# A fused attention, DFT and MLP kernel: front-end steps, weight sums and the start of TensorE's fixed order moved by a few matmul groups

## The chip, the cores and the metric

One core of one Trainium2 chip. The core's engines run side by side, each through its own queue in order: TensorE (PE) for matrix products, VectorE (DVE), ScalarE (ACT) and GpSimd (POOL) for elementwise work, SyncE (SP), which issues nearly all the DMAs here. The metric is the device time of one execution in microseconds; lower is better.

## What is computed

Pooled attention over 8 batches and 8 heads, then per batch a two-dimensional Fourier transform of which only the real part is kept, a layer norm, and an MLP of 512, 2048 and 512 channels.

```python
# q, k, v: (8, 8, 576, 64); pool = 8; w_ch1: (512, 2048); w_ch2: (2048, 512)
k_p = k.reshape(B, H, Sp, pool, D).mean(axis=3)
v_p = v.reshape(B, H, Sp, pool, D).mean(axis=3)
scores = scale * np.matmul(q, k_p.transpose(0, 1, 3, 2))
scores = scores - np.max(scores, axis=-1, keepdims=True)
attn = np.exp(scores)
attn = attn / (np.sum(attn, axis=-1, keepdims=True) + 1e-09)
attn_out = np.matmul(attn, v_p)            # -> x: (8, 576, 512)
...
X = np.fft.fft(np.fft.fft(x, axis=1), axis=2)
u = x + np.real(X).astype(np.float32)
mu = np.mean(u, axis=-1, keepdims=True)
var = np.mean((u - mu) ** 2, axis=-1, keepdims=True)
un = (u - mu) / np.sqrt(var + 1e-06)
return u + np.maximum(un @ w_ch1, 0.0) @ w_ch2
```

## The kernel before

**Two streams of work.** The MLP runs over nine blocks of 512 tokens, 4608 tokens in all; since a batch has 576 tokens, each block takes its tokens from two neighbouring batches, the last of one and the first of the next. The generator `fast()` yields the MLP's matmuls in 920 groups, mostly four to six matmuls each; a group's number is called its position here. Blocks 0 and 1 (`plain`, from positions 0 and 93) multiply the normalised tokens with the first weight in split precision: twelve matmuls into one PSUM tile g (L889), on the high part un0h, the low part un0l and un0h again; relu on ACT gives hh, DVE gives the low part hl (L895), and the second product collects in acc0 to acc3 (L853). From block 2 on (position 189, 104 positions to a block) the first product is made by a scheme with seven half-size products in place of eight (x, L957), which DVE adds up (sx, L918); ACT makes relu and hh (L926, L927), POOL hl (L928).

**The front end.** `fe(b)` is a generator too: all that batch b needs before its tokens can enter the MLP. In its order: pooling of k and v as trees of adds on POOL (L360); scores psS on TensorE (L432), their maxima mx on DVE (L434), the exps on ACT (L439); transposes psT, psV, psR; attention times values, psX (L516), which ACT copies into the batch's tile U (L518, L519) and DVE adds up in pairs (L526, L527); even and odd parts tmpE (L610) and tmpO (L623), split into high and low parts f (L600, L602); the transform's products psA (L644), psB (L661), psQ and psP; the mean psM (L755 to L760), the variance psVar (L806 to L825), the inverse root and the multiplication X (L833); and last the MLP's operands, un0l and un1l, on DVE and POOL (L725, L736, L739).

**What joins them.** The front end is cut into some 48 steps by its `yield`s. A table (AT for batches 4 to 7, AT3, AT2 and AT1) gives for each step the position behind which it is emitted, counted from the start of a block (`start`, `places`, `advance`). A step that is emitted sooner stands sooner on every engine on which its instructions run. MANUAL is the position from which TensorE executes exactly in the order in which the program is written; before it, and on the other engines all along, a scheduler sets the order.

**Weight sums.** The scheme of blocks 2 to 8 needs sums and differences of weight blocks. `combine(j)`, j from 0 to 7, makes them in one tile sx: four adds on DVE over the pair loaded from DRAM (L230 to L233), a high part on ACT (L236) and a low part on POOL (L237) for each of two halves, four stores to w1s (L239), and behind them the load of the next pair (L224) into the tile that the stores have just read. PAIRS gives their positions.

**Buffers.** PSUM has eight banks. Four are acc0 to acc3. Until block 0 is written, the others are two for g and two for the front end; then the program closes that pool and opens one ring of four that g, x and the front end share in turn. A tile takes the next bank of the ring, and waits until what was in it has been read. Weight tiles of the stream go round in a ring of twelve, loaded up to nine ahead by SP. Three tiles U hold batches in turn, `Us[b % 3]`; `evict` adds acc into U and sends it out (L874 to L879).

Of the kernel before, what the change touches and what calls it, by code (L numbers as in the profile page):

```python
# [52 lines left out]

RES = [0, 3, 6, 9, 11, 14]

UNITS0, UNITS, MANUAL, TAIL = 90, 104, 92, (2, 8, 14, 20, 26)
PAIRS = [97 + 11 * n for n in range(8)]
AT = [-64, -58, -56, -52, -50, -38, -36, -33, -31, -28, -26, -8, -6, 13, 14, 15, 16, 17, 18, 21, 22, 25, 26, 27, 28, 28,
      40, 41, 44, 46, 48, 49, 52, 52, 53, 55, 57, 59, 65, 66, 66, 79, 80, 80, 81, 82, 82, 104]
AT3 = [-46, -40, -38, -34, -32, -20, -18, -15, -14, -11, -9, -6, -4, 13, 14, 15, 16, 17, 18, 21, 22, 25, 26, 27, 28, 28,  # L60
      40, 41, 44, 46, 48, 49, 52, 52, 53, 55, 57, 59, 65, 66, 66, 79, 80, 80, 81, 82, 82, 104]
AT2 = [-6, 2, 4, 6, 8, 17, 18, 21, 22, 23, 24, 26, 27, 28, 29, 30, 31, 33, 34, 37, 38, 41, 42, 43, 44, 44,
       53, 54, 56, 57, 59, 60, 61, 61, 62, 64, 65, 66, 69, 70, 70, 79, 80, 80, 80, 81, 81, 100]
AT1 = [-1] * 7 + [2 + 3.5 * n for n in range(17)] + [93, 101, 113, 116, 117, 117, 117]
E0, O0, E1, O1 = 0, 1, 2, 3

HB = BLK // 2
# [17 lines left out]
def tile_kernel(ctx: ExitStack, tc: tile.TileContext, qt, kt, vm, vr, w1, w2, cad, cbd, mkd, out):  # L85
# [180 lines left out]
    def feed(look):  # L266

        while flow[1] < min(len(items), flow[0] + look):
            x = items[flow[1]]
            t = fresh("w1op" if x[0] in "ap" else "w2high" if x[0] == "h" else "w2low")  # L270
            if x[0] == "p":
                nc.sync.dma_start(raw(t), w1p[:, x[1], x[2]])
            elif x[0] != "a":
                nc.sync.dma_start(raw(t), (w2d if x[0] == "h" else w2l)[:, x[2]])
            else:
                src = w1s[:, x[2], x[3] - 3] if x[3] > 2 else w1p[:, 2 * x[2] + x[3] // 2, :, (x[3] > 0) * HB:(x[3] > 0) * HB + HB]
                nc.sync.dma_start(raw(t).rearrange("p (a n) -> p a n", a=2), src)
            tiles[x] = t
            flow[1] += 1
# [720 lines left out]
    def prep_next():  # L1000
        prep_w(done[0])
        done[0] += 1
# [4 lines left out]
        return UNITS0 + 96 * (k - 1) + (UNITS - 96) * max(0, k - 2) if k else 0  # L1007

    def places(c):
        return {1: AT1, 2: AT2, 3: AT3}.get(c, AT)  # L1010

    def advance(pos):
        for c in sorted(run):
            r = run[c]
            at = places(c)
            while r[1] < len(at) and pos >= at[r[1]] + start(c - 1):
                r[1] = len(at) - 1 if next(r[0], None) == "ln" else r[1] + 1
        c = max(run) + 1
        if c < B and pos + 1 >= places(c)[0] + start(c - 1):
            run[c] = [fe(c), 0]  # L1020
# [4 lines left out]
    for pos, _ in enumerate(fast()):  # L1025
        if pos % 3 == 2 and done[0] < min(len(pieces), AHEAD + pos // 3):
            prep_next()
        if pos in PAIRS:
            combine(PAIRS.index(pos))
        if pos in TAIL:  # L1030
            next(fe0, None)
        advance(pos)
        if done[0] == len(pieces):
            held = len(lows) + sum(i == 1 and f not in RES for i, f in highs)
            feed(LOOK if not held else min(LOOK, WBUFS - 3 - held))
        if pos + 1 == MANUAL:
            ctx.enter_context(tc.manual_schedule(engines={mybir.EngineType.PE}))
# [109 lines left out]
```

## Time and profile before

| | us |
|---|---|
| median of 3 runs | 1065.73 |
| lowest, highest run | 1061.01, 1066.77 |
| span of the profiled execution | 1062.5 |
| TensorE busy in it | 1004.7 (95%) |
| VectorE, ScalarE, GpSimd busy | 700.9 (66%), 567.1 (53%), 445.2 (42%) |

The profile was taken in one execution, of which the span is the time from its first to its last instruction; its whole time is not recorded apart, so the span is set beside the three timed runs. Busy times are read per engine: an engine that is busy for 95% of the span is short of work for 5% of it, and the views below say where. A row of the waits reads "line of the waiting instruction, from whose result it was released, total, times, longest". In a timeline a bracket at a row's end gives the idle time of the engine just before it and what ended that. The granted clock of TensorE is 1.00 at 2.4 GHz and 0.50 at 1.2 GHz.

### The profile page before, as it was taken

How to read it: one execution, taken by the hardware profiler on the slowest of the kernel's cores; microseconds unless marked ns; L12 is line 12 of the kernel's file. 1: busy time of each engine (PE TensorE's matmuls, PEld its weight loads, DVE VectorE, ACT ScalarE, POOL GpSimd, SP SyncE). 2: the span in 40 equal slices, each digit the busy share in tenths (PEclk: the TensorE clock that was granted, in tenths of full speed). 3: DMA queues.
4: the chain of work that ended last, by engine and by line, in shares of the span. 5: the costliest groups of instructions: out<-in, count | busy, mean ns of one | idle time of the engine just before them, and what ended most of it. 6: DMA issues, size and time to landing. Idle time of an engine off the chain costs nothing.

```text
span 1062.5 us, 18758 instructions
## 1 busy us (share of the span) xinstructions
PE 1004.7 (95%) x5982; PEld 868.1 (82%) x5982; DVE 700.9 (66%) x1387; ACT 567.1 (53%) x1687; POOL 445.2 (42%) x461
## 2 busy tenths in 40 slices
PE   6879999898898899999999999999999999999998
PEld 4656778677777789888998889889989998999997
DVE  6898686766579657866786667866785677223222
ACT  5768673565445655565557556566655344222221
POOL 5614433245533564357534753454352234222221
PEclk8989999899899999999999999999999999999999
DMA  8479997687755776777677767786777588988883
GB/s 274 176 236 393 357 326 245 200 258 242 244 158 151 248 253 197 244 248 260 206 236 256 246 194 232 236 268 202 219 224 242 168 247 258 298 256 261 290 257 136
DMA packets 161458, 256.11 MB, mean 241 GB/s; under 512 B 15952, under 2 KB 73296, under 8 KB 161104
## 3 DMA queue, kind: packets, MB, share of 16 engines
q1 hardware_dynamic: 161072, 252.24, 73.8%
q0 software_dynamic: 288, 2.66, 0.7%
q8 instruction: 49, 0.80, 0.3%
q14 instruction: 49, 0.40, 0.1%
HBM read 217.63 MB, written 37.22 MB: 240 GB/s over the span
## 4 chain that ended last, share of the span: by engine, by line
PE 66%; DVE 10%; DMA 9%; POOL 6%; ACT 5%; issue 3%; SPq 0%; POOLq 0%; DVEq 0%; ACTq 0%
PE acc L853 28%; PE x L957 21%; PE g L889 4%; PE psX L516 3%; DMA v<-in_vm 2%; DMA k<-in_kt 2%; ACT t L439 2%; PE psS L432 2%; PE psP L678 2%; DMA sx<-w1d 1%; PE psT L468 1%; PE psB L661 1%; DMA w1s<-sx 1%; PE psA L644 1%; POOL v L360 1%
## 5 line engine op out<-in xcount | busy, mean ns | idle before, releaser
L918 DVE TENSOR_TENSOR sx<-x,sx 128x256 f32<-128x256 f32 x336 | 154.5, 464 | 144.4 <-PE x L957 139.5
L928 POOL TENSOR_TENSOR hl<-sx,hh 128x512 fp32r<-128x512 f32 x112 | 153.9, 1374 | 222.3 <-ACT hh L927 196.5
L957 PE MATMUL x<-un0h,w1op 128*128 128x256 f32 x896 | 174.4, 282 | 0.2 <-ACT t L439 0.2
L853 PE MATMUL acc<-hh,w2low 128*128 128x512 f32 x576 | 165.1, 400 | 0.0
L926 ACT ACTIVATE sx<-sx 128x512 f32<-128x512 f32 x112 | 71.0, 634 | 156.9 <-DVE sx L918 154.8
L957 PEld LDWEIGHTS x<-un0h,w1op 128*128 128x128 f32 x896 | 143.4, 189 | 11.6 <-ACT t L439 0.4
L957 PE MATMUL x<-un1h,w1op 128*128 128x256 f32 x672 | 134.2, 281 | 2.7 <-DVE A L629 1.6
L957 PEld LDWEIGHTS x<-un1h,w1op 128*128 128x128 f32 x672 | 111.5, 188 | 17.0 <-DVE sx L918 3.0
L853 PEld LDWEIGHTS acc<-hh,w2low 128*128 128x128 f32 x576 | 101.2, 189 | 15.9 <-issue 0.4
L853 PE MATMUL acc<-hh,w2high 128*128 128x512 f32 x360 | 106.7, 405 | 0.0
L853 PE MATMUL acc<-hl,w2high 128*128 128x512 f32 x360 | 104.3, 399 | 2.3 <-POOL hl L928 2.3
L957 PE MATMUL x<-un0l,w1op 128*128 128x256 f32 x448 | 88.9, 280 | 3.3 <-DVE un0l L736 3.3
L439 ACT ACTIVATE t<-psS,mx 128x72 f32<-128x72 f32 x240 | 73.9, 333 | 17.9 <-DVE mx L434 17.5
L853 PEld LDWEIGHTS acc<-hl,w2high 128*128 128x128 f32 x360 | 63.2, 189 | 13.8 <-POOL hl L928 4.1
L853 PEld LDWEIGHTS acc<-hh,w2high 128*128 128x128 f32 x360 | 64.4, 192 | 9.4
L927 ACT CAST hh<-sx 128x512 fp32r<-128x512 f32 x112 | 69.8, 624 | 3.0
L957 PEld LDWEIGHTS x<-un0l,w1op 128*128 128x128 f32 x448 | 68.2, 188 | 3.8 <-DVE un0l L736 3.7
L360 POOL TENSOR_TENSOR v<-v 128x256 f32<-128x256 f32 (+1 forms) x56 | 53.7, 959 | 37.6 <-DMA v<-in_vm 36.7
L957 PE MATMUL x<-un1l,w1op 128*128 128x256 f32 x336 | 66.4, 279 | 1.1 <-POOL un1l L736 1.1
L853 PE MATMUL acc<-hl,w2h 128*128 128x512 f32 x216 | 61.3, 403 | 2.0 <-DVE hl L895 1.4
L448 POOL TENSOR_TENSOR t<-t,sm 128x720 f32<-128x720 f32 x30 | 45.3, 1512 | 42.7 <-DVE sm L447 21.4
L853 PE MATMUL acc<-hh,w2h 128*128 128x512 f32 x216 | 60.4, 399 | 1.8 <-ACT hh L927 1.2
(267 smaller groups left out, 2096.1 us busy)
## 6 DMA issues: line engine op xcount, KB each, us to landing
w1op<-w1s SPq DMA_DIRECT2D x224, 256.0 KB, 3.4
w1op<-w1p SPq DMA_DIRECT2D x200, 256.0 KB, 3.7
w2low<-w2l SPq DMA_DIRECT2D x128, 256.0 KB, 3.7
w2high<-w2d SPq DMA_DIRECT2D x80, 256.0 KB, 3.7
U<-in_w SPq DMA_DIRECT2D x16, 512.0 KB, 6.0
sx<-in_w SPq DMA_DIRECT2D x16, 512.0 KB, 5.9
w1s<-sx SPq DMA_DIRECT2D x32, 256.0 KB, 3.8
k<-in_kt SPq DMA_DIRECT2D x28, 288.0 KB, 3.3
```

The lines of the kernel that those rows point to most:

```text
L360: nc.gpsimd.tensor_tensor(out=out if n == 1 else src[:, :, 0:n], in0=src[:, :, 0] if n == 1 else src[:, :, 0:n], in1=src[:, :, 1] if n == ...
L432: nc.tensor.matmul(ps[:, c * W2J:(c + 1) * W2J], lhsT=q[:, r0:r0 + P], rhs=kpb[g % 2], start=True, stop=True)
L439: behind["S", b, gi, i] = nc.scalar.activation(t[:, c0 + c, h], pv[:, c, h], AF.Exp, bias=mx[x], accum_out=sm[x])
L448: ins = nc.gpsimd.tensor_tensor(out=t, in0=t, in1=sm.unsqueeze(3).broadcast_to([P, 5, 2, J]), op=ALU.mult)
L516: behind["X", b] = nc.tensor.matmul(ps, lhsT=w, rhs=a, start=(i == 0), stop=(i == len(mm) - 1))
L853: nc.tensor.matmul(acc[e], lhsT=a[:, e], rhs=h, start=(f == 0 and x == 0), stop=(f == NFC - 1 and x == 2))
L889: nc.tensor.matmul(ps, lhsT=w[:, c], rhs=x[:, ti], start=(n == 0), stop=(n == 11))
L918: nc.vector.tensor_tensor(out=o, in0=x, in1=y, op=ALU.add)
L926: nc.scalar.activation(c, c, AF.Relu)
L927: nc.scalar.copy(out=h, in_=c)
L928: nc.gpsimd.tensor_tensor(out=l, in0=c, in1=raw(h), op=ALU.subtract)
L957: nc.tensor.matmul(ps, lhsT=w[:, q, i], rhs=y[:, c + i], start=(n == 0), stop=(n == 5))
```

## The change

It moves the emission of steps; no instruction's work changes. MANUAL goes from 92 to 86. PAIRS, eight positions 11 apart, become a list in which sums 3 and 4 share position 136. AT1, AT2 and AT3 are rewritten, and AT is replaced by one table for each of the batches 4 to 7. Line numbers of the changed kernel are 8 higher than before.

```diff
-UNITS0, UNITS, MANUAL, TAIL = 90, 104, 92, (2, 8, 14, 20, 26)
-PAIRS = [97 + 11 * n for n in range(8)]
-AT = [-64, -58, -56, -52, -50, -38, -36, -33, -31, -28, -26, -8, -6, 13, 14, 15, 16, 17, 18, 21, 22, 25, 26, 27, 28, 28,
...
+UNITS0, UNITS, TAIL = 90, 104, (2, 8, 14, 20, 26)
+MANUAL = 86
+PAIRS = [95, 110, 119, 136, 136, 145, 158, 174]
+AT4 = [-64, -58, -56, -46, -46, -38, -36, -33, -31, -28, -27, -9, -7, 13, 15, 15, 16, 17, 18, 21, 22, 25, 26, 27,
...
     def places(c):
-        return {1: AT1, 2: AT2, 3: AT3}.get(c, AT)
+        return (None, AT1, AT2, AT3, AT4, AT5, AT6, AT7)[c]
...
-        if pos in PAIRS:
-            combine(PAIRS.index(pos))
+        for j, p in enumerate(PAIRS):
+            if p == pos:
+                combine(j)
```

In positions: batch 2's four score tiles of its first group of heads go from 92, 94, 96 and 98 to 96, 98, 98 and 98; its psA steps (s26 to s28) from 143, 144 and 146 to 142 for all; the steps with psM to the end by one up or down. Batch 3's score steps s9 to s12 go from 175, 177, 180 and 182 to 179 for all, its psX steps s13 to s16 from 199 to 202 to 199 for all, s21 to s25 from 211 to 214 to 207 for all; s28 stands at 221 (before 230) and s29 at 227 (before 232). In batches 4 to 7 the second pair of score steps stands 6 and 4 positions later, the middle of the transform one later, and the last six steps, at 79 to 82 of their block before, all at 76 now.

TensorE, where block 1 begins: psS_3 and psS_2 are score tiles of batch 2, g_1_0 the first tile of block 1. Before:

```order
L853 MATMUL acc_3_887<-hl,w2h 128x512
L432 MATMUL psS_3_0_1865<-kpb_79,q_3_1793 128x144 x3
L889 MATMUL g_1_0_1881<-un0h_870,w1op 128x512 x4
L889 MATMUL g_1_0_1881<-un0l_871,w1op 128x512 x4
L432 MATMUL psS_3_3_1901<-kpb_79,q_3_1793 128x144 x2
L889 MATMUL g_1_0_1881<-un0h_870,w1op 128x512 x4
L853 MATMUL acc_0_884<-hh,w2high 128x512
L853 MATMUL acc_0_884<-hh,w2low 128x512
L853 MATMUL acc_0_884<-hl,w2high 128x512
L853 MATMUL acc_1_885<-hh,w2high 128x512
L432 MATMUL psS_2_0_1954<-kpb_78,q_2_1807 128x144 x3
```

The first three score products stand ahead of g_1_0, two more inside it.

TensorE at the same place in the changed kernel:

```order
L861 MATMUL acc_3_887<-hl,w2h 128x512
L897 MATMUL g_1_0_1876<-un0h_850,w1op 128x512 x4
L897 MATMUL g_1_0_1876<-un0l_851,w1op 128x512 x4
L897 MATMUL g_1_0_1876<-un0h_850,w1op 128x512 x4
L861 MATMUL acc_0_884<-hh,w2high 128x512
L861 MATMUL acc_0_884<-hh,w2low 128x512
L861 MATMUL acc_0_884<-hl,w2high 128x512
L861 MATMUL acc_1_885<-hh,w2high 128x512
L440 MATMUL psS_3_0_1915<-kpb_79,q_3_1793 128x144 x3
```

After eight further products into acc, TensorE's order in the changed kernel goes on with the rest of the scores, the first tile of block 1's second piece of the hidden layer (g_1_1) and psVar of batch 1:

```order
L440 MATMUL psS_3_3_1938<-kpb_79,q_3_1793 128x144 x2
L440 MATMUL psS_2_0_1979<-kpb_78,q_2_1807 128x144 x3
L440 MATMUL psS_2_3_1990<-kpb_78,q_2_1807 128x144 x2
L897 MATMUL g_1_1_2059<-un0h_850,w1op 128x512 x4
L897 MATMUL g_1_1_2059<-un0l_851,w1op 128x512 x4
L814 MATMUL psVar_2072<-avg,lf 128x1 x5
```

The scores have gone from in front of and between the parts of g_1_0 to behind it, four tiles close together ahead of g_1_1, and psVar of batch 1 stands one third of g_1_1 sooner.

DVE, around weight sum 5 (the rows on sx are its four adds) and the psX adds of batch 2. Before:

```order
L526 TENSOR_TENSOR U_86<-psX_0_2540,U_86 128x288
L895 SCALAR_TENSOR_TENSOR hl<-g_1_6_2506,hh 128x512
L527 TENSOR_TENSOR U_86<-psX_0_2540,U_86 128x288
L526 TENSOR_TENSOR U_86<-psX_0_2551,U_86 128x288
L527 TENSOR_TENSOR U_86<-psX_0_2551,U_86 128x288
L610 TENSOR_TENSOR tmpE<-U_86 128x287
L410 SCALAR_TENSOR_TENSOR rw_80<-vt,mk,rw_80 32x63
L410 SCALAR_TENSOR_TENSOR rw_80<-vt,mk,rw_80 32x1
L616 TENSOR_TENSOR xt<-U_86 1x287
L623 TENSOR_TENSOR tmpO<-U_86 128x288
L526 TENSOR_TENSOR U_86<-psX_1_2566,U_86 128x288
L230 TENSOR_TENSOR sx<-sx 128x256
```

The sum's first add is the last of these rows.

DVE at that place in the changed kernel:

```order
L508 TENSOR_TENSOR R<-psR_1_2500,R 32x512
L903 SCALAR_TENSOR_TENSOR hl<-g_1_6_2495,hh 128x512
L534 TENSOR_TENSOR U_86<-psX_0_2531,U_86 128x288
L535 TENSOR_TENSOR U_86<-psX_0_2531,U_86 128x288
L238 TENSOR_TENSOR sx<-sx 128x256
L534 TENSOR_TENSOR U_86<-psX_0_2546,U_86 128x288
L239 TENSOR_TENSOR sx<-sx 128x256
L534 TENSOR_TENSOR U_86<-psX_1_2553,U_86 128x288
L535 TENSOR_TENSOR U_86<-psX_0_2546,U_86 128x288
L618 TENSOR_TENSOR tmpE<-U_86 128x287
```

The sum's first add has gone from behind both psX_0 adds, tmpE, xt, tmpO and the first psX_1 add to a place between the two pairs of psX_0 adds.

DVE, where the operands of block 2 are made (un0l_2295 before, un0l_2276 now; un0l_3420 belongs to block 3). Before:

```order
L434 TENSOR_REDUCE mx<-psS_1_0_3331 128x6
L447 RECIPROCAL sm<-sm 128x10
L736 TENSOR_TENSOR un0l_2295<-X,un0h_2294 128x4x192
L434 TENSOR_REDUCE mx<-psS_1_3_3354 128x4
L739 TENSOR_TENSOR X<-X 128x2x192 x4
L446 TENSOR_SCALAR sm<-sm 128x10
L447 RECIPROCAL sm<-sm 128x10
L895 SCALAR_TENSOR_TENSOR hl<-g_1_15_3366,hh 128x512
L736 TENSOR_TENSOR un0l_3420<-X,un0h_3419 128x4x96
L736 TENSOR_TENSOR un0l_2295<-X,un0h_2294 128x4x192
```

The second un0l_2295, the last row, stands behind hl and un0l_3420.

DVE there in the changed kernel:

```order
L903 SCALAR_TENSOR_TENSOR hl<-g_1_14_3276,hh 128x512
L442 TENSOR_REDUCE mx<-psS_0_0_3300 128x6
L442 TENSOR_REDUCE mx<-psS_0_3_3311 128x4
L744 TENSOR_TENSOR un0l_2276<-X,un0h_2275 128x4x192
L442 TENSOR_REDUCE mx<-psS_1_0_3327 128x6
L442 TENSOR_REDUCE mx<-psS_1_3_3338 128x4
L747 TENSOR_TENSOR X<-X 128x2x192 x3
L454 TENSOR_SCALAR sm<-sm 128x10
L747 TENSOR_TENSOR X<-X 128x2x192
L455 RECIPROCAL sm<-sm 128x10
L744 TENSOR_TENSOR un0l_2276<-X,un0h_2275 128x4x192
```

The block's second un0l has lost the other block's un0l and an hl in front of it, and two maxima of score tiles stand further forward.

## Rows read from the trace of the kernel before

**Rows 1.** The page's first line: the span of the profiled execution.

```profile
span 1062.5 us, 18758 instructions
```

**Rows 2.** Stretches: window, length, busy us by engine, TensorE's clock, DMA share, GB/s.

```profile
186.00:235.00 49.00, 41.91 (x203) 33.65 (x202) 35.00 (x77) 28.63 (x122) 16.80 (x15) 0.93 0.71 230
235.00:335.00 100.00, 90.09 (x452) 74.52 (x451) 66.93 (x130) 56.26 (x202) 45.14 (x53) 0.95 0.67 211
335.00:400.00 65.00, 57.53 (x373) 50.98 (x372) 41.37 (x91) 34.73 (x115) 36.30 (x45) 0.97 0.71 225
400.00:880.00 480.00, 471.62 (x3101) 424.29 (x3100) 348.80 (x688) 275.31 (x863) 220.48 (x215) 1.00 0.73 229
192.80:199.60 6.80, 4.01 (x10) 3.27 (x11) 4.04 (x10) 4.16 (x17) 4.01 (x4) 0.50 0.34 115
264.50:271.30 6.80, 3.33 (x11) 2.86 (x12) 4.91 (x7) 1.88 (x5) 4.87 (x7) 0.50 0.49 135
281.50:284.90 3.40, 3.40 (x13) 2.91 (x12) 2.25 (x5) 2.87 (x12) 3.24 (x5) 0.50 0.52 124
339.50:343.00 3.50, 3.50 (x11) 2.72 (x10) 2.55 (x10) 1.02 (x2) 1.31 (x1) 0.51 0.26 77
```

**Rows 3.** TensorE's waits, 180 to 1050 us: line, released by, total us, times, longest.

```profile
PE psA L644 <- DVE f L602: 4.7, 1, 4.7
PE g L889 <- ACT t L439: 4.5, 1, 4.5
PE x L957 <- DVE un0l L736: 3.3, 2, 3.0
PE acc L853 <- POOL hl L928: 2.9, 4, 1.0
PE psS L432 <- ACT t L439: 2.4, 1, 2.4
PE x L957 <- DVE A L629: 1.6, 1, 1.6
PE psX L516 <- ACT U L519: 1.6, 1, 1.6
PE psB L661 <- ACT f L600: 1.4, 1, 1.4
```

**Rows 4.** TensorE's timeline, 187 to 214 us: start, duration, instruction, idle before it and releaser.

```profile
195.59 2.08 PE L889 MATMUL g<-un0h,w1op 128*128 128x512 f32 x4 [4.51 <-ACT t L439]
197.46 1.91 PE L889 MATMUL g<-un0l,w1op 128*128 128x512 f32 x4
```

**Rows 5.** DVE's timeline, 186 to 197 us, the last un0l of block 1.

```profile
194.97 0.31 DVE L725 TENSOR_TENSOR un0l<-X,un0h 128x160 fp32r<-128x160 f32 x1
```

**Rows 6.** ACT's timeline, 190 to 197 us, the last exp of the first score tile.

```profile
195.10 0.34 ACT L439 ACTIVATE t<-psS,mx 128x72 f32<-128x72 f32 x1
```

**Rows 7.** DVE's timeline, 240 to 270 us, around weight sum 5 and batch 2's f.

```profile
252.66 0.44 DVE L623 TENSOR_TENSOR tmpO<-U 128x288 f32<-128x288 f32 x1
...
258.60 0.42 DVE L230 TENSOR_TENSOR sx<-sx 128x256 f32<-128x256 f32 x1 [5.13 <-POOL wlo L401]
...
261.90 1.29 DVE L232 TENSOR_TENSOR sx<-sx 128x256 f32<-128x256 f32 x1
263.12 3.50 DVE L623 TENSOR_TENSOR tmpO<-U 128x288 f32<-128x288 f32 x1
...
267.47 0.82 DVE L602 TENSOR_TENSOR f<-tmpE,f 128x290 fp32r<-128x290 f32 x2
```

**Rows 8.** SP's timeline, 236 to 262 us: weight loads and the request of sum 5's pair.

```profile
248.13 0.98 SPq L272 DMA_DIRECT2D w1op<-w1p  x2
...
252.75 0.32 SPq L224 DMA_DIRECT2D sx<-w1d  x1
```

**Rows 9.** POOL's timeline, 242 to 268 us: the first of the trees over v and k.

```profile
261.77 1.14 POOL L360 TENSOR_TENSOR v<-v 128x256 f32<-128x256 f32 x1 [3.83 <-DMA v<-in_vm]
```

**Rows 10.** DVE's timeline, 326 to 341 us, the two un0l ahead of block 2.

```profile
334.89 3.99 DVE L736 TENSOR_TENSOR un0l<-X,un0h 128x384 fp32r<-128x384 f32 x2
```

More of the change, by code (lines that the diff above doesn't have):

```diff
@@ L54 @@
 RES = [0, 3, 6, 9, 11, 14]
-UNITS0, UNITS, MANUAL, TAIL = 90, 104, 92, (2, 8, 14, 20, 26)
-PAIRS = [97 + 11 * n for n in range(8)]
-AT = [-64, -58, -56, -52, -50, -38, -36, -33, -31, -28, -26, -8, -6, 13, 14, 15, 16, 17, 18, 21, 22, 25, 26, 27, 28, 28,
-      40, 41, 44, 46, 48, 49, 52, 52, 53, 55, 57, 59, 65, 66, 66, 79, 80, 80, 81, 82, 82, 104]
-AT3 = [-46, -40, -38, -34, -32, -20, -18, -15, -14, -11, -9, -6, -4, 13, 14, 15, 16, 17, 18, 21, 22, 25, 26, 27, 28, 28,
-      40, 41, 44, 46, 48, 49, 52, 52, 53, 55, 57, 59, 65, 66, 66, 79, 80, 80, 81, 82, 82, 104]
@@ L62 @@
-AT2 = [-6, 2, 4, 6, 8, 17, 18, 21, 22, 23, 24, 26, 27, 28, 29, 30, 31, 33, 34, 37, 38, 41, 42, 43, 44, 44,
-       53, 54, 56, 57, 59, 60, 61, 61, 62, 64, 65, 66, 69, 70, 70, 79, 80, 80, 80, 81, 81, 100]
-AT1 = [-1] * 7 + [2 + 3.5 * n for n in range(17)] + [93, 101, 113, 116, 117, 117, 117]
+UNITS0, UNITS, TAIL = 90, 104, (2, 8, 14, 20, 26)
+MANUAL = 86
+PAIRS = [95, 110, 119, 136, 136, 145, 158, 174]
+AT4 = [-64, -58, -56, -46, -46, -38, -36, -33, -31, -28, -27, -9, -7, 13, 15, 15, 16, 17, 18, 21, 22, 25, 26, 27,
+       28, 29, 41, 42, 45, 49, 49, 50, 53, 53, 54, 55, 58, 60, 65, 65, 65, 76, 76, 76, 76, 76, 76, 104]
@@ new lines @@
+AT5 = [-64, -58, -56, -46, -46, -38, -36, -33, -31, -28, -27, -9, -7, 13, 15, 15, 16, 17, 18, 21, 22, 25, 26, 27,
+       28, 29, 41, 42, 45, 47, 49, 49, 49, 53, 54, 55, 58, 60, 65, 65, 65, 76, 76, 76, 76, 76, 76, 104]
+AT6 = [-64, -58, -56, -46, -46, -38, -36, -33, -31, -28, -27, -10, -7, 13, 15, 15, 16, 17, 18, 21, 22, 25, 26, 26,
+       28, 29, 41, 42, 45, 47, 49, 50, 53, 53, 54, 55, 58, 60, 65, 65, 65, 76, 76, 76, 76, 76, 76, 104]
+AT7 = [-64, -58, -56, -46, -46, -38, -36, -33, -31, -28, -27, -11, -11, 13, 13, 13, 13, 17, 18, 21, 22, 25, 26, 27,
+       28, 29, 41, 42, 45, 47, 49, 50, 53, 53, 54, 55, 58, 60, 65, 65, 65, 76, 76, 76, 76, 76, 76, 104]
@@ new lines @@
+AT3 = [-46, -40, -37, -33, -33, -20, -18, -15, -15, -7, -7, -7, -7, 13, 13, 13, 13, 15, 15, 17, 18, 21, 21, 21, 21,
+       21, 34, 35, 35, 41, 42, 43, 47, 47, 48, 51, 52, 54, 60, 61, 61, 74, 75, 75, 76, 78, 78, 104]
+AT2 = [-6, 6, 8, 8, 8, 17, 18, 21, 22, 23, 24, 26, 27, 27, 29, 31, 32, 34, 35, 38, 39, 42, 43, 43, 44, 44, 52, 52,
+       52, 57, 59, 60, 61, 61, 61, 63, 65, 66, 70, 70, 70, 78, 78, 78, 78, 78, 80, 99]
+AT1 = [-2, -2, -2, -2, -2, -2, 2, 2, 4.5, 8.0, 12.5, 16.0, 19.5, 23.0, 24.5, 28.0, 32.5, 35.0, 42.5, 42.5, 45.5,
+       49.0, 53.5, 57.0, 92, 100, 111, 114, 115, 115, 116]
```

## The prediction, made before the changed kernel had run

> **What bounds the kernel now.** The span is 1062.5 us [rows 1]. I read the busy time by stretch first, cut where the moved steps lie [rows 2]: idle is window minus PE busy, so 49.00 - 41.91 = 7.1 us in 186 to 235, 9.9 in 235 to 335, 7.5 in 335 to 400 and 480.00 - 471.62 = 8.4 in 400 to 880, together 32.9 us. Elsewhere behind 186 TensorE works without a pause that counts: it is the bound, and the change, which alters no arithmetic, can win only this idle time and the stretches in which its clock was low. What is idle before 186 lies ahead of every step whose move can matter, and is left out. Four short windows in the same group show a granted clock of 0.50, the lower of TensorE's two levels (1.2 instead of 2.4 GHz), each behind or around one of these waits. TensorE was busy in them for 4.01 + 3.33 + 3.40 + 3.50 = 14.2 us; at the upper level the same work takes half, so about 7.1 us more can be had. The prize is thus 32.9 + 7.1 = 40 us, 3.8%, and no more. Second, who ended each idle stretch [rows 3]: five waits of 1.6 to 4.7 us, all in the hand-over from block 0 to block 1 and in the front ends of batches 2 and 3, carry about half of it. All else is a crumb.
>
> **Block 1's first group (A).** Before, two score tiles psS of batch 2 were emitted at group 92, in front of the first group of block 1. At group 93 the banks of PSUM change hands, and that group waited 4.51 us for the last of six exps on ACT [rows 3], which ends at 195.44 [rows 6]; TensorE restarts at 195.59 [rows 4]. After the change the scores stand at groups 96 and 98, so the bank is free. What is late next are block 1's own operands: the last un0l on DVE runs 194.97 to 195.28 [rows 5]. That piece is needed by the group's eighth matmul alone. Four matmuls took 197.46 - 195.59 = 1.87 us at the low clock [rows 4], so 0.93 at the upper and 1.6 for seven; the first can then stand at 195.3 - 1.6 = 193.7, 1.9 us earlier, and with half of the 4.01 us at the low clock 3.9 are to be had. Against it: four psS tiles now stand in groups 96 to 98 of a ring of four banks, and group 99 needs a bank again. Their 20 exps at 0.34 us [rows 6] are 6.8 us of ACT, against 6 groups of 0.93 us between 93 and 99, 5.6 us: the scores need 1.2 us more than there is, and a bank is asked for before the last of them. I let 2.2 us come back as a new wait: -1.7, bounds -3.9 to 0.
>
> **The weight sums and batch 2's psA (C), batch 3's psS (D).** The third matmul of psA waits 4.67 us for f on DVE [rows 3], whose two instructions start at 267.47 [rows 7]. Back along DVE: it stood idle for 5.13 us ahead of the first add of weight sum 5 (L230, started 258.60), because the pair it adds was asked of the DMA at 252.75 [rows 8] and was there 5.8 us later; that request waits on SP for the stores of the sum before. DVE executes in order, so psX adds, tmpE, tmpO and f all stood behind. The change emits sums 3 and 4 both at group 136 and sum 5 at 145. The order of DVE then has the sum's first add between the psX_0 adds, 7 rows earlier, so seven more instructions of about 0.44 us stand behind it (3.1 us). The request stands two weight loads earlier on SP, between the two issued from 248.13 on [rows 8], so it can go out up to 4 us sooner, if the stores before it are through; I take 3. From the first add to the end of f it took 268.29 - 258.60 = 9.7 us; in it are two stretched instructions, 3.50 us where the same tmpO took 0.44, and 1.29 for a 0.42 add: 3.9 us. Without them 5.8, plus 3.1 is 8.9 us. With the pair there at 255.5, f ends at 264.4 and psA gains 3.9 us; with it there at 258.5 and stretched as before f ends at 271.3. D is a chain of its own: the second k of batch 3 arrives late, and six exps ahead of the bank give a 2.4 us wait; its load now stands on SP behind the sum's request, which argues against a gain, its psS bank is freed one group later, which argues for little. For both together I take -4.3: 3.9 less a small new wait, plus half of the low clock behind psA (1.7), less 1 to 1.5 for D's worse place. Bounds: -10.5 (all of 4.7 + 2.4 and the clock's 1.7 + 1.7) to +5 (DVE's 5.13 us now lands on TensorE, see the rivals).
>
> At this place the trace shows POOL's trees starting at 261.77 [rows 9] and DVE's two-input adds stretching in the same microseconds. The Trainium skill (SBUF — State Buffer, Who interferes with whom) says that a DVE instruction with two SBUF inputs contends with a GpSimd instruction that reads SBUF, and that the loser fully blocks; the trace agrees, 3.50 against 0.44 us. By that rule the gain hangs on whether DVE's adds are through before the trees begin; it makes a rival of its own below.
>
> **psVar, psM and psB (B).** The smaller waits in 186 to 335 come to 17.0 - 4.5 - 4.7 - 2.4 = 5.4 us. Batch 1's last steps move up by 1 to 2 groups and batch 2's psM down by 1, so some of these waits shorten and some don't: -1.0, bounds -2.7 (half of them) to 0.
>
> **Block 2's first products (F).** TensorE waits 3.0 us [rows 3] for un0l, the operand's low half. DVE runs two un0l in a row there for 3.99 us [rows 10]; the first is another block's and has half the elements, a third of the two, 1.3 us. After the change it no longer stands in front, and psVar of batch 2, with which the chain to un0l begins, starts two groups (1.9 us) sooner: 1.3 + 1.9 = 3.2 us earlier, less the reductions mx of two more score tiles that come in between, so the wait is all but gone, and with it most of the 1.7 us of low clock behind it. -4.0, bounds -4.7 to -1.5.
>
> **Batch 3's psX and psB (G, H).** psX waits 1.6 us for ACT's copy into U [rows 3], a copy that overwrites what the output DMA of batch 0 still reads. The change puts all four psX at group 199, 0 to 3 groups sooner, but the DMA lands when it lands, and after the change a product at group 202 needs the bank: 0, bounds -1.6 to +2 (three groups of 0.93 less slack). psB waits 1.4 us for f; s28 to s29 stand six groups apart instead of two: -1.4, bounds -1.4 to 0.
>
> **Blocks 4 to 7 (late).** 8.4 us idle, two thirds of it at the blocks' starts, where hl on POOL (2.9 us in four waits) or un1l comes late because the operands of the next batch fill POOL and DVE. The six last steps of each batch now stand at 76 instead of 79 to 82, 3 to 6 groups or 3 to 6 us sooner, more than the longest wait of 1.6. I count half: -4.2, bounds -8.4 to +1.6 (one more wait as long as the longest there).
>
> **New rows of equal steps.** At 136, 142, 179, 199, 207 and 366 the table now puts two to six steps at one group. Each such row needs its banks at once from a ring of four; I have no row of it but the waits for banks in G and D. +3.0, bounds 0 to +6 (two as long as D's and a half). The earlier start of the written order (group 86 instead of 92) moves no instruction of TensorE, which stands in the same order there in both programs: 0.
>
> **Sum.** -1.7 - 4.3 - 1.0 - 4.0 + 0 - 1.4 - 4.2 + 3.0 = -13.6. Ends: -3.9 - 10.5 - 2.7 - 4.7 - 1.6 - 1.4 - 8.4 + 0 = -33.2, and 0 + 5 + 0 - 1.5 + 2 + 0 + 1.6 + 6 = +13.1. The span of 1062.5 becomes 1048.9; the median of the runs shown, 1065.73, is 3.2 above the span, so 1052.1. I say 1052.
>
> **Rivals.** (1) The trees meet DVE again: the adds still run while POOL works, 3.9 us come back, the sum is -9.7 and the time 1056. For: POOL has the same trees there, and they start when their loads land, which move up with the rest. Against: the adds start up to 3 us sooner, ahead of 261.77. (2) Everything moved is covered and nothing new is late: some -28, 1038. Against: it needs six steps at one group to cost nothing. (3) Gains eaten: the sums' load comes no sooner, C and D give 0, the rings cost 6, the late blocks give 2: -1.7 + 0 - 4.0 + 6 - 2.0 = -1.7, 1064. For: sum 3 moved six groups later, and each sum's request waits for the stores of the one before. (4) Slower: DVE's wait for the pair now begins with one psX_0 and both psX_1 still unread, three of four banks; if the pair comes after 259.5, no gain is left in psA (259.5 + 8.9 = 268.4), and TensorE itself stops for a bank. Price +5 there, +6 in the rings, -1.5 in F, nothing elsewhere: +9.5, 1075. It decides from a load that lands 1 us later than the 258.5 of before. That the change does nothing at all is out: the orders differ on every engine.
>
> **How the numbers follow.** A measurement of this kernel can tell about 0.5%, 5.3 us, from no change: faster is under 1060.4, slower over 1071.1. The forecast 0.44, (1) 0.15 and (2) 0.06 are faster, 0.65; (3) 0.20 is the same; (4) 0.15 is slower. The range 1040 to 1072 leaves out (2) and nearly all of (4), 0.20 together.
>
> **What would show it.** In the profile after: g of block 1 waits under 2 us for ACT's t; DVE's first add of sum 5 starts before 256 and psA's longest wait is under 1.5; x no longer waits for un0l at block 2; hl's waits sum to under 1.5 us; the low-clock windows near 265 and 340 are gone. I am wrong if TensorE shows waits for psX or psS banks of over 3 us in 245 to 260 or around block 2, or if POOL's trees still stretch tmpO.

## The result, and the profile after

The changed kernel takes 1051.65 us (median of 4 runs, 1049.36 to 1052.21), against 1063.99 for the kernel before (4 runs on the same chip, 1061.01 to 1066.77). The ratio is 0.9882, with a 95% interval of 0.985 to 0.9913: 1.2% or 12.5 us less. The forecast was 1052, in a range of 1040 to 1072. The profiled execution took 1051.85 us, 1.75 more than its span.

The first lines of the page of the changed kernel, which answer to [rows 1]; the last is TensorE's granted clock in 40 slices:

```profile
span 1050.1 us, 18757 instructions
...
PE 1003.6 (96%) x5982; PEld 866.0 (82%) x5982; DVE 692.2 (66%) x1387; ACT 566.7 (54%) x1687; POOL 440.7 (42%) x461
...
PEclk8989999899899999999999999999999999999999
```

TensorE is busy for nearly as long as before, 1003.6 us against 1004.7; what shrank is the rest of the span, from 57.8 to 46.5 us. TensorE's waits, 180 to 1050 us, which answer to [rows 3] (line, released by, total us, times, longest):

```profile
PE psA L652 <- ACT f L608: 3.6, 1, 3.6
PE psS L440 <- DVE U L704: 2.3, 1, 2.3
PE g L897 <- DVE X L770: 2.1, 1, 2.1
PE x L965 <- ACT U L527: 1.6, 1, 1.6
PE g L897 <- DVE hl L903: 1.1, 2, 0.6
PE x L965 <- DVE sx L926: 1.1, 2, 0.6
PE psS L440 <- DVE sx L926: 1.1, 1, 1.1
PE acc L861 <- ACT hh L935: 1.1, 3, 0.4
```

Of the five long waits of before, psA's is left in place, now 3.6 us, and psX's for ACT's copy into U at group 202 (1.6) has become x's for the same copy at the same group (1.6). The wait of block 1's first tile for ACT's exps (4.5), that for un0l at block 2 (3.0), that of psS for the exps (2.4) and all four waits for POOL's hl (2.9) are gone. In their place stand two of about 2 us that before did not show: psS for DVE's U, and g for DVE's X.

Of the signs that the forecast named, four came: g of block 1 waits 0.6 us for ACT's exps, sum 5's first add starts at 254.05, and the waits for un0l at block 2 and for hl are gone. Two did not: psA still waits 3.6 us, and the clock is low from 263.3 to 270.2 and from 348.7 to 352.1.

Where the gain arises is read by setting the two traces side by side: when TensorE starts the same group. The column e12 is the same reading of a run from the experiments below, whose rows stand in the order of before on every engine until 534 us, behind group 366: what it shows up to there is by how much two executions of the same code differ.

| from group to group | lead of the changed kernel at its end, us | gained in the stretch | e12 | forecast |
|---|---|---|---|---|
| 0 to 92 | 0.7 | 0.7 | 0.6 | 0 |
| 92 to 140 (A, part of B) | -0.4 | -1.1 | 0.3 | A 1.7 |
| 140 to 152 (C, D) | 3.4 | 3.9 | 2.9 | 4.3 |
| 152 to 189 (rest of B) | 2.4 | -1.0 | -3.4 | B 1.0 |
| 189 to 200 (F) | 5.3 | 2.9 | 0.0 | 4.0 |
| 200 to 230 (G, new rows of steps) | 3.2 | -2.1 | 0.3 | -3.0 |
| 230 to 235 (H) | 5.7 | 2.6 | -0.2 | 1.4 |
| 235 to 293 | 8.9 | 3.2 | 0.0 | 0 |
| 293 to the end (late) | 12.4 | 3.5 | | 4.2 |

Two things keep the single rows from being read as terms. The 3.9 us of 140 to 152 are mostly the trace of before, which was slow there in that execution: e12 gains 2.9 in the same stretch without any change (e1, e2 and e11, unchanged up to there as well, 3.5 to 4.2), and gives 3.4 back by 189. And from 189 to 293 the cuts run through steps that moved: 25 more matmuls of the front end stand between 189 and 230 in the changed kernel and 25 fewer between 230 and 293, so the loss of 2.1 and the gains behind it are in part the same work on the other side of a cut. Three long stretches can be compared. From 92 to 189 (A to D) 1.8 us were gained and 7.0 forecast; from 189 to 293 (F, G, H and the new rows) 6.5 gained and 2.4 forecast; behind it 3.5 gained and 4.2 forecast. The sum is right within 2 us (-13.6 forecast). Its parts are not, and that is what the experiments had to take apart.

### The profile page after: what moved, and what is told of

The parts are those of the page before. It is cut to its first block, busy times and chain, and to the rows that moved or that the text cites. A ratio compares the mean times of both kernels' runs of the same rounds, so it can differ in the third digit from the quotient of the medians.

```text
span 1050.1 us, 18757 instructions
## 1 busy us (share of the span) xinstructions
PE 1003.6 (96%) x5982; PEld 866.0 (82%) x5982; DVE 692.2 (66%) x1387; ACT 566.7 (54%) x1687; POOL 440.7 (42%) x461
## 4 chain that ended last, share of the span: by engine, by line
PE 76%; DVE 9%; DMA 7%; ACT 3%; POOL 2%; issue 2%; SPq 1%; DVEq 0%; POOLq 0%; ACTq 0%
PE acc L861 33%; PE x L965 23%; PE g L897 6%; PE psX L524 3%; PE psS L440 3%; DMA sx<-w1d 2%; PE psP L686 2%; DMA w1s<-sx 2%; PE psA L652 1%; ACT t L447 1%; PE psT L476 1%; PE psB L669 1%; PE psQ L686 1%; DMA v<-in_vm 1%; DMA k<-in_kt 1%
## 5 line engine op out<-in xcount | busy, mean ns | idle before, releaser
L936 POOL TENSOR_TENSOR hl<-sx,hh 128x512 fp32r<-128x512 f32 x112 | 150.8, 1347 | 225.7 <-ACT hh L935 184.0
L965 PEld LDWEIGHTS x<-un1h,w1op 128*128 128x128 f32 x672 | 111.2, 189 | 13.6 <-DVE sx L926 2.0
```

What stands on the lines that cost most here:

```text
L936: nc.gpsimd.tensor_tensor(out=l, in0=c, in1=raw(h), op=ALU.subtract)
L965: nc.tensor.matmul(ps, lhsT=w[:, q, i], rhs=y[:, c + i], start=(n == 0), stop=(n == 5))
```

## Experiments

Each kernel was timed against the kernel before on the same chip; a ratio below 1 is faster, and 0.001 is 1.06 us. Lines of a kernel's own are a few off those of before, because its tables have other lengths.

### The four parts alone

The diff is one table of the change at a time, put into the kernel before:

```diff
 e1: PAIRS -> [95, 110, 119, 136, 136, 145, 158, 174]
 e2: AT    -> AT4, AT5, AT6, AT7
 e3: AT1, AT2 -> the new AT1, AT2
 e4: AT3   -> the new AT3
```

> The kernel before with the new positions of the eight weight sums alone; all front-end tables as before. Theory S (the change is a sum of local effects, each where its steps lie): sum 5's pair is asked for some 3 us sooner and DVE's first add starts before 256, but its adds meet POOL's trees, so psA's wait stays over 2.5 us; psS of batch 3 keeps its wait of 2.4. Time -1 us (-3 to +2) against before. Rival W (the weight sums are what carried the change): -5 us or more. Rival T (the parts only work together): slower than before by 2 us or more.

> The kernel before with the new tables of batches 4 to 7 alone. Theory S: the two traces part by 6.2 us more between position 240 and the end (from -6.2 at 240 to -12.4 at 916), all of it in these tables' stretch, so this alone gives -6.2 us (-7.5 to -4.5), and the idle time of TensorE from 400 to 880 us falls from 8.4 to under 3 us. Rival W: within 2 us of before. Rival T: under half of it, -3 or less.

> The kernel before with the new tables of batches 1 and 2 alone (scores of batch 2 behind block 1's first group, psA at 142). Theory S: between positions 92 and 146 the two traces stand 0.9 us apart to the worse, the wait of 4.5 us at block 1's first group coming back as later waits; psVar of batch 2 two groups sooner gives some at block 2: -1 us (-3 to +1.5). Rival A (the removed wait at block 1 is kept): -4 or more. Rival T: slower than before by 2 or more.

> The kernel before with the new table of batch 3 alone. Theory S: psB's wait of 1.4 us and what goes with it is gone (the traces part by 2.6 us between 230 and 235), four score tiles at 179 take the other un0l from in front of block 2's (up to 3 us and 1.7 of low clock), four equal steps at 199 and 207 cost 2.5 back: -3 us (-5.5 to 0). Rival T: within 1 of before or slower.

| alone | ratio, 95% interval | us |
|---|---|---|
| weight sums | 1.0009, 0.9995 to 1.0023 | +1.0 |
| batches 4 to 7 | 0.9963, 0.9947 to 0.9978 | -3.9 |
| batches 1 and 2 | 0.9937, 0.9917 to 0.9958 | -6.7 |
| batch 3 | 0.9963, 0.9947 to 0.9978 | -3.9 |

The four add up to -13.5 us, known to some 3.5 us by their intervals, and the whole change gave -12.5: neither rival W nor T holds, and theory S, a sum of effects that each lie where their steps are, fits. It is not proved by the sum, since one gain is in two of the parts (below). Three sizes were far off. The weight sums, in whose earlier place the forecast saw most of C, give nothing. Batches 4 to 7 give 3.9 us where S had 6.2, outside its range, and TensorE's idle time from 400 to 880 us falls from 8.4 to 7.05 us, not under 3. And batches 1 and 2, which I had put at -1, carry half of the gain. Their waits in 240 to 345 us, of the kernel with these two tables alone, show it against [rows 3]:

```profile
PE psA L649 <- ACT f L605: 2.7, 1, 2.7
PE psS L437 <- DVE U L701: 2.1, 1, 2.1
PE acc L858 <- DVE U L882: 0.8, 1, 0.8
```

The wait for un0l at block 2 is not among them. Batch 3's table alone takes it away too, and with it the wait for un1l at block 3's start (1.1 us, which the forecast had put down to the tables of batches 4 to 7; those alone take it away as well). TensorE's waits in 325 to 480 us of that kernel:

```profile
PE x L961 <- ACT U L523: 1.8, 1, 1.8
PE psS L436 <- DVE hl L899: 1.3, 1, 1.3
PE acc L857 <- POOL hl L932: 0.6, 1, 0.6
PE psT L472 <- DVE sx L922: 0.2, 1, 0.2
```

No un0l, no un1l; new are psS (1.3) at the four equal steps of group 179 and x (1.8) behind those of group 199. So F is a gain that two parts can each make, and that counts once in the whole. From 189 to 293, against the trace of before, e3 gains 5.0 us, e4 6.6 and the whole change 6.5.

### Scores and last steps of batch 2

```diff
 e8:  AT2: -6, 2, 4, 6, 8,   ->  -6, 6, 8, 8, 8,       (first five steps only)
 e11: AT2: 69, 70, 70, 79, 80, 80, 80, 81, 81, 100
        -> 70, 70, 70, 78, 78, 78, 78, 78, 80, 99      (last ten steps only)
```

> The kernel before with nothing moved but batch 2's first four score steps, from groups 92, 94, 96, 98 to 96, 98, 98, 98. Theory S: the wait of 4.5 us at block 1's first group falls to about 2.1 (for X, the mean subtracted) and the rest comes back by group 118, so 0 us (-2 to +2) and the gain of batches 1 and 2's tables (7 us) lies in later steps. Rival A: this alone gives over 4 of the 7 us.

> The kernel before with nothing moved but batch 2's last ten steps (s38 to s47: psM, psVar, the inverse root, the operands), most of them one or two groups sooner. Theory F (a sooner psVar takes the wait for un0l away): un0l's wait of 3.0 us falls under 1 and the low-clock window behind it goes, 2 to 4.5 us faster than before. Rival G (the wait goes only where four score tiles or the steps before shift too): un0l's wait stays over 2, the time within 1.5 us of before.

The scores alone give 0.9998 (0.9979 to 1.0017): nothing, within 2 us. TensorE's timeline of that kernel where block 1 begins, only the rows with idle time before them (start, duration, instruction, idle and releaser), shows how 4.51 us can go without any gain:

```profile
190.10 0.71 PE L893 MATMUL g<-un0h,w1op 128*128 128x512 f32 x2 [2.10 <-DVE X L766]
191.19 0.74 PE L893 MATMUL g<-un0h,w1op 128*128 128x512 f32 x2 [0.38 <-ACT un0h L728]
192.21 0.73 PE L893 MATMUL g<-un0l,w1op 128*128 128x512 f32 x2 [0.28 <-DVE un0l L729]
193.68 0.73 PE L893 MATMUL g<-un0l,w1op 128*128 128x512 f32 x2 [0.74 <-DVE un0l L729]
...
201.34 1.20 PE L893 MATMUL g<-un0h,w1op 128*128 128x512 f32 x4 [0.76 <-ACT t L443]
```

The tile starts at 190.10 instead of 195.59, because it waits for X alone. Then it stops three times more for pieces of its own operands, and the next tile once for a bank behind the scores, 4.26 us in all; the score products that stood in front are now paid behind. The change moved TensorE's idle time, and the engines that feed it (ACT with the exps, DVE with X and un0l) needed as long as ever.

The last ten steps alone give 0.9966 (0.9948 to 0.9985), -3.6 us, within theory F. DVE's timeline of that kernel, with the un0l that answers to [rows 10]:

```profile
324.10 0.96 DVE L740 TENSOR_TENSOR un0l<-X,un0h 128x768 fp32r<-128x768 f32 x1
...
330.30 0.96 DVE L740 TENSOR_TENSOR un0l<-X,un0h 128x768 fp32r<-128x768 f32 x1
...
332.29 0.63 DVE L740 TENSOR_TENSOR un0l<-X,un0h 128x384 fp32r<-128x384 f32 x1
```

The un0l of block 2 (128x768) ends at 331.26, with the other block's (128x384) behind it, and takes 0.96 us; TensorE shows no wait for it at block 2. Term F is thus confirmed in place and size, 4.0 forecast, 3.6 measured. Its low-clock part is not: the granted clock of this kernel is 0.50 for 3.4 us as before, now from 343.9 to 347.3; in return psX's wait of 1.6 us is gone.

The cause, too, is wider than the forecast had it. The same line before, in 326 to 340 us (each engine's shortest, median and longest instruction in ns, first and last start), first on DVE, then on POOL:

```profile
L736 DVE TENSOR_TENSOR un0l<-X,un0h x3: 895/1519/2553, 328.8 to 336.3; 128x768 fp32r<-128x768 f32 x2, 128x384 fp32r<-128x384 f32 x1
L736 POOL TENSOR_TENSOR un1l<-X,un1h x3: 916/1643/2115, 328.9 to 335.9; 128x384 fp32r<-128x384 f32 x1, 128x192 fp32r<-128x192 f32 x1, 128x768 fp32r<-128x768 f32 x1
```

The un0l for which TensorE waited started at 336.3, beside POOL's un1l of 335.9, and took 2.55 us instead of 0.96; the other block's ahead of it took 1.52 instead of 0.63. So some 2.5 of the 3.99 us in [rows 10] come from running beside POOL. In e11 the un0l of block 2 is done before POOL starts its own large un1l at 332.47. How much of the gain is this, and how much the other block's un0l and the sooner psVar, was not tried apart. What the steps between (psT to psP of batch 2, and batch 1's) give, about 3 us of the 6.7, was not tried by itself.

### psA, weight sum 5 and POOL's trees

> The changed kernel, leaving out two of the three levels of the pooling trees over v and its remainder for batches 3 and 4 (two of eight rows are added), so that POOL reads little while DVE prepares batch 2's f. Theory P (DVE is stretched by POOL's reads): tmpE falls from 1.89 to about 0.45 us and xt from 1.40 to 0.45, f ends 2 to 3 us sooner and psA's wait falls from 3.6 to under 1.7 us; the whole is 2 to 5 us faster. Rival Q (the wait comes from the queue of rows behind the sum's load alone): tmpE stays over 1.5, psA's wait over 3, the time within 1 us.

The diff leaves two levels of the trees away in two batches:

```diff
-            for n in (4, 2, 1):
+            for n in (1,) if b in (3, 4) and out.shape[-1] == D else (4, 2, 1):
```

First DVE's timeline of the changed kernel, which answers to [rows 7], then POOL's beside it:

```profile
250.86 0.46 DVE L535 TENSOR_TENSOR U<-psX,U 128x288 f32<-128x288 f32 x1
254.05 0.43 DVE L238 TENSOR_TENSOR sx<-sx 128x256 f32<-128x256 f32 x1 [2.73 <-DMA sx<-w1d]
...
257.86 1.40 DVE L624 TENSOR_TENSOR xt<-U 1x287 f32<-1x287 f32 x1
...
259.92 0.96 DVE L241 TENSOR_TENSOR sx<-sx 128x256 f32<-128x256 f32 x1
...
262.21 1.89 DVE L618 TENSOR_TENSOR tmpE<-U 128x287 f32<-128x287 f32 x1
...
264.98 1.43 DVE L610 TENSOR_TENSOR f<-tmpE,f 128x290 fp32r<-128x290 f32 x2
```

```profile
257.65 1.29 POOL L245 TENSOR_TENSOR sx<-sx 128x512 f32<-128x512 f32 x1 [0.55 <-DVE sx L240]
258.90 1.70 POOL L368 TENSOR_TENSOR v<-v 128x256 f32<-128x256 f32 x1
...
261.94 0.62 POOL L368 TENSOR_TENSOR v<-v 128x128 f32<-128x128 f32 x1
262.52 1.25 POOL L245 TENSOR_TENSOR sx<-sx 128x512 f32<-128x512 f32 x1
263.74 0.52 POOL L368 TENSOR_TENSOR vs<-v 128x64 f32<-128x64 f32 x1
```

The pair of sum 5 comes 4.5 us sooner than before (254.05 against 258.60, asked for at 248.94 instead of 252.75), more than I had taken. But xt takes 1.40 us, tmpE 1.89 where the first tmpE took 0.44, the sum's last add 0.96 and f 1.43 instead of 0.82. So f is done at 266.41, 1.9 us sooner than in the trace of before, and TensorE still waits for it, 3.6 us for f's high part on ACT, which tmpE holds up, and 0.4 for its low part. This is the first rival of the forecast, the trees meeting DVE again, at about the price that it gave (3.9 us; here 1.0 for xt, 1.4 for tmpE, 0.5 for the add and 0.6 for f, 3.5). Only tmpO, which the forecast had named, was spared (0.44).

The trace of before is one execution, and a bad one here. In five runs whose order up to this place is that of before (e1, e2, e4, e11, e12) tmpO takes 0.45 to 1.39 us, not 3.50, f is done at 265.3 to 267.5, not at 268.29, and psA waits 3.4 to 5.6 us in all (before 5.7). Four runs with the new order (the changed kernel, e3, e5, e9) wait 2.9 to 4.0. So psA gained about 1 us, and most of its pair's lead (4.5 us on the trace of before, 2.1 to 3.8 on those five) was lost again on DVE.

With the trees cut short the ratio is 0.9826 (0.9799 to 0.9853), 5.9 us under the changed kernel's 0.9882. But the changed kernel was not run beside it. What ran beside it, on the same chip, was e5, which is the changed program itself (next section), at 0.9833: by that pair the probe gives 1.2 us (1045.67 against 1046.88). What it is worth, some 1 to 6 us, stays open. DVE and POOL of that kernel:

```profile
257.34 1.40 DVE L624 TENSOR_TENSOR xt<-U 1x287 f32<-1x287 f32 x1
...
261.13 1.34 DVE L618 TENSOR_TENSOR tmpE<-U 128x287 f32<-128x287 f32 x1
...
263.35 0.82 DVE L610 TENSOR_TENSOR f<-tmpE,f 128x290 fp32r<-128x290 f32 x2
```

```profile
257.13 1.29 POOL L245 TENSOR_TENSOR sx<-sx 128x512 f32<-128x512 f32 x1 [0.55 <-DVE sx L240]
...
260.88 1.27 POOL L245 TENSOR_TENSOR sx<-sx 128x512 f32<-128x512 f32 x1
```

f is back at 0.82 and starts 1.6 us sooner, and psA's wait falls to 1.8 us, where the three executions of the changed program show 2.9 to 4.0. tmpE stays at 1.34, not the 0.45 that theory P wanted, and xt at 1.40: what is left beside them on POOL is sum 5's own subtraction (L245), and both end 0.32 us behind it. That POOL's rows stretch DVE's is borne out by f and by psA's wait, and rival Q's marks (tmpE over 1.5, psA over 3) did not come; but P's own marks for tmpE and xt were missed, since the weight sum brings a POOL reader of its own, and the time does not decide between the two. By group 189 the gain at psA is gone again: from 140 to 189 this kernel gains 4.2 us on the trace of before, the executions of the changed program 2.9 to 4.4.

### The weight sums undone, and the changed kernel again

```diff
 e5:  PAIRS -> [97 + 11 * n for n in range(8)]    (in the changed kernel)
 e9:  no difference to the changed kernel
```

> The changed kernel with the old positions of the weight sums. Theory S (local effects that add): the sums alone cost 1 us, so without them 1051 us, within 1.5 of the changed kernel, and psA's wait for f is 2.5 to 3.5 us, as with batches 1 and 2 alone. Rival C (the new sums are needed by the new tables): slower than the changed kernel by 3 us or more, with psA's wait or a new DVE wait for the pair over 5 us.

> The changed kernel itself once more, on the same chip as the next three. All theories: a ratio of 0.988 to the kernel before (0.985 to 0.991). If it comes out near 0.984, the gain that seemed to lie in undoing the weight sums was a difference between chips.

Without the new positions of the sums the ratio is 0.9833 (0.9803 to 0.9862; runs from 1044.53 to 1052.58, before at 1062.98). The changed kernel, run again beside e10 to e12, came out at 0.988 (0.9857 to 0.9904). So the new positions are not needed, against rival C. Nor are the old ones better. Set side by side row by row, the traces of e5 and of the changed kernel hold the same instructions in the same order on all five engines (5982 rows on TensorE, 1387 on DVE, 1687 on ACT, 461 on POOL, 923 on SP), and e1's are in the order of the kernel before. The positions in PAIRS, moved like this, change nothing that runs: DVE's scheduler sets the adds of sum 5 between the psX_0 adds in both kernels, and what shifted that was batch 2's table. So e1 is the kernel before once more (+1.0 us), and e5 the changed kernel a third time: 0.9882, 0.988 and 0.9833, 5 us apart, are what measurements of one program differ by here. The waits of e5 in 240 to 330 us are of the same kind:

```profile
PE psA L652 <- ACT f L608: 2.5, 1, 2.5
PE psS L440 <- DVE U L704: 1.6, 1, 1.6
```

### Waits covered by moving their waiters

```diff
 e7:  AT2: 44, 44, 52, 52, 52, 57   ->  44, 44, 56, 56, 56, 57
 e10: PAIRS as in e5; AT2: 44, 44, 55, 55, 55, 58
      AT3: -37, -33, -33 -> -37, -31, -31;  13, 13, 13, 13, 15 -> 13, 16, 16, 17, 17
```

> The changed kernel with batch 2's three psA steps at group 146 instead of 142, as they were before the change give or take three groups. Theory S: four groups of 0.93 us cover the 3.6 and 0.4 us that TensorE waits for f; the wait and most of the low-clock window near 265 go: 3 to 5.5 us faster than the changed kernel, 1046 to 1049. Rival R (the chain behind psA to psM, psVar and un0l is what counts and starts as late as before): within 1 us, with longer waits for psP, psM or un0l.

> The changed kernel with the old positions of the weight sums, batch 2's psA steps at 145 and the first psB step at 148, batch 3's score steps s3 and s4 at 155 and its psX steps at 199, 202, 202 and 203. Theory S (each wait is a local one and can be covered by moving its waiter): psA's 3.6 + 0.4 us falls under 1.5, psS's 2.3 under 1, the 1.65 us of x for the copy behind the output DMA under 0.5, and the low-clock windows near 265 and 350 go: 5 to 9 us faster than the changed kernel. Rival R (the chains behind are what counts, the wait turns up again at the next consumer): within 3 us of it, with new waits for psB, psM or un0l.

Both were meant to beat the changed kernel, and neither does: 0.9875 (0.9843 to 0.9907) and 0.9885 (0.9853 to 0.9918). TensorE's waits of the second in 180 to 400 us:

```profile
PE psB L669 <- DVE f L610: 3.0, 2, 2.8
PE g L897 <- DVE X L770: 2.1, 1, 2.1
PE g L897 <- DVE hl L903: 1.4, 2, 0.8
PE psS L440 <- DVE R L508: 1.4, 1, 1.4
PE psM L768 <- DVE shl L718: 1.1, 1, 1.1
PE psV L488 <- ACT U L530: 1.1, 1, 1.1
```

psA's wait is down to 0.9 us, psS's for U and x's for the copy are gone, as wished. psB now waits 2.8 us, psM 1.1, psV 1.1, and TensorE's pauses of over 0.2 us from 180 us on sum to 23.2 us against 21.6 in the changed kernel (22.3 in e9). In e7 psA waits no more, but psB waited 2.5 us for A and 1.3 for f. A, which psB follows, stood on DVE behind sum 6's add, which waited for its pair (2.84 us): a new collision, and not only the old chain. Rival R holds in both by the time and the new waits. That DVE's chain from psX to psM is the bound here, and TensorE's waits only show where it surfaces, fits e10; it was not tried by shortening that chain.

### The last six steps of batches 4 to 7

```diff
 e12: AT: 79, 80, 80, 81, 82, 82 -> 76, 76, 76, 76, 76, 76
```

> The kernel before with nothing moved but the last six steps of batches 4 to 7, all at 76 of their block. Theory L (operands made sooner free POOL and DVE before the next block): the waits for hl and un1l (2.9 + 1.1 us) go, most of the 3.9 us that the whole tables give alone: -3 us (-4.5 to -1.5). Rival M (the gain of these tables lies in the steps of the middle): within 1 us of before.

The ratio is 0.9979 (0.9962 to 0.9996), -2.2 us of the -3.9 that the whole tables give: within theory L, at its lower end, but the interval reaches into rival M's 1 us as well. The waits for hl fall from 2.9 us to 2.0, not away, and un1l's 1.1 us stays; with the whole tables alone hl's fall to 0.9 and un1l's is gone, so the later middle steps help there.

This kernel has a second use: no engine's order in it differs from the one before until 534 us, long past block 2's start. Its waits in 200 to 300 us:

```profile
PE psA L649 <- DVE f L607: 5.3, 2, 4.1
PE psP L683 <- DVE U L701: 1.4, 1, 1.4
...
PE psS L437 <- ACT t L444: 0.7, 1, 0.7
```

In the same code the waits of before show 4.7 for psA and 2.4 for psS [rows 3], none for psP, and a second one for psA:

```profile
PE psA L644 <- ACT f L600: 1.0, 1, 1.0
```

One execution moves 1 to 2 us from one of these waits to another; their sum is 7.7 us here and 8.1 there. In the changed kernel it is 6.3 (psA 4.0, psS 2.3). The low clock moves as well: before it was low from 281.5 to 284.9 behind psS [rows 2], here it is behind psM, where TensorE waits for shl (0.7 and 1.4 us):

```profile
301.50:304.90 3.40, 3.40 (x11) 2.73 (x10) 2.63 (x4) 0.54 (x2) 1.78 (x2) 0.50 0.27 78
```

The changed kernel has neither of the two windows, and no wait for psM.

## Why the prediction was right, and where it was not

**What bounds the kernel.** Right. TensorE's busy time stayed, and 11.3 of the 12.4 us between the two spans are idle time. What A, C and F had counted on from the low clock did not come in this execution: behind 186 us TensorE was busy for 14.5 us in the three low-clock windows of the changed kernel, 14.2 in the four before. A second execution (e9) has two windows, of 6.8 and 3.4 us, so what the clock gives back is not settled.

**A, forecast -1.7, measured about 0.** The wait went and another came, as said; the step that failed is "I let 2.2 us come back". All of it came back, within the 2 us that e8 can tell. The bound on the first matmul was wrong as well: it started at 190.93 in the changed kernel, not at 193.7 at the earliest, as soon as X and the first un0h were there. But starting sooner only meant stopping at each operand (the last un0l was done at 194.46, 0.8 us sooner than before), and at the low clock, as this stretch of the changed kernel shows (window, length, busy us by engine, clock, DMA share, GB/s), which answers to [rows 2]:

```profile
191.70:198.50 6.80, 6.22 (x13) 4.19 (x14) 3.52 (x9) 3.60 (x8) 4.11 (x4) 0.50 0.35 100
263.30:270.20 6.90, 4.89 (x20) 4.29 (x21) 3.97 (x7) 1.84 (x5) 5.46 (x9) 0.51 0.82 259
348.70:352.10 3.40, 3.40 (x14) 2.86 (x13) 1.84 (x4) 2.14 (x8) 1.91 (x2) 0.50 0.60 173
```

**C and D, forecast -4.3, 3.9 between the two traces.** Right by its number alone, and by luck. The mechanism (the new positions of the sums bring the pair sooner) is refuted: those positions change no order (e1, e5). The pair did come sooner, by batch 2's table, and the first rival's collision ate most of it at psA, with the clock low for as long as before in this execution (263.30). The price of C was also read off one execution, with a tmpO of 3.50 us that five others of the same order do not show. Nor does the gain lie at D: a wait of 2.3 us for psS, before at group 148, stands at group 153 now, behind the cut, and e12 gains 2.9 in 140 to 152 without a change.

**B, forecast -1.0.** With C and D, from 140 to 189, the changed kernel gains 2.9 us on the trace of before, and e12 loses 0.5: some 3 us, of which psM's waits (2.1) and the low-clock window behind them are the part that can be named. From 92 to 140, A's stretch, it loses 1.1, with new waits of g for hl (1.1) and of psS for R (1.0); psVar's new waits for qhl at group 168 take 1.3. All in all A to D brought 1.8 us of the 7.0 forecast.

**F, forecast -4.0.** Right in place and size (e11: -3.6). The cause was named in part: un0l was also held beside POOL's un1l, and a third of 3.99 us, 1.3, is not what the other block's un0l costs (0.63 where nothing holds it). What the forecast missed besides is that batch 3's table does the same again.

**G, forecast 0.** Right, in the form that it named: "a product at group 202 needs the bank". The wait is 1.65 us instead of 1.56.

**New rows, forecast +3.0.** This term was off by about all of its size. TensorE's idle time from 200 to 230 fell from 3.1 to 2.3 us, with 13 more matmuls of the front end in the stretch; in the whole change no wait for a bank stands behind these rows but G's. Without this term F, G and H come to -5.4, and 6.5 us were gained from 189 to 293.

**H, forecast -1.4.** psB's wait of 1.4 us is gone; what lies behind it can't be told from F by the cuts.

**The late blocks, forecast -4.2, measured -3.5 between the traces and -3.9 alone (e2).** Right in size. The cause was right for about half of it: the last six steps, on which the forecast counted, give 2.2 us (e12), and the middle steps, for which it had counted nothing, the rest.

**MANUAL.** In e3, which has 92, every engine's order is that of the changed kernel until 275 us, where batch 3's table sets in; so 86 moves nothing there. In the kernel before no run shows it.

The total was right because errors of several us of both signs cancelled: A to D brought 5.2 us less than forecast, and F to H with the new rows 4.1 more. What the chances rested on, that several independent local gains stand against a few new waits, is borne out by batch 2's last steps (e11), batch 3's table (e4) and the late blocks (e2). About 3 us of batches 1 and 2's 6.7 were not traced to a step.

## What to carry to other kernels

When an engine's wait is taken away by moving the waiter, look up what the feeding engines need from that point to the next consumer: if their chain is no shorter, the wait comes back there (e7, e8, e10). Gains that stay are those where the chain itself begins sooner or loses a row in front of it (e11, and with less certainty e12). And a step's place in the program sets its place only on the engine whose order is written; on the others look at the order that results, and test a table entry alone before giving it a share of the sum: the new PAIRS changed no row. Last, a term read off a single execution can be an accident of it. Set a second execution of the same code beside it, as e12 is here, before a stretch of the trace is put down to an edit.

## What the runs showed of the hardware

DVE adds with both inputs in SBUF can be held by POOL's reads for longer than one POOL instruction. In the changed kernel tmpE starts at 262.21 under POOL's v (261.94 to 262.56) and is still held through the subtraction that follows at once (262.52 to 263.77); it ends at 264.10, 0.33 us behind it. The 3.50 us of tmpO before [rows 7] are of this kind. It is no rule: xt ends 0.32 us behind its subtraction (at 258.94), although POOL's v follows as closely (258.90), and there it is v that gets longer, 1.70 us where [rows 9] has 1.14. What decides which of the two goes first, no run here shows. The Trainium skill (SBUF — State Buffer, Summary: rules for kernel authors) says that, where DVE has two SBUF inputs and the GpSimd instruction reads SBUF, the second of the two to issue blocks until the first finishes. These rows agree for one instruction (xt) and show a hold through two in a row (tmpE).
